# Squared scores of the first chunk stored unturned, read back in 256-byte pieces and turned in four later chunks

## The chip, the cores and the metric

One core of one Trainium2 chip runs the kernel. The metric is device time in microseconds (us); it is 1084.96 us before the change, the median of three runs (1084.34 to 1086.16).

## The reference, cut to what matters

Three layers follow each other over two samples of 3136 tokens. The change touches the first, an attention without softmax:

```python
def _attn_ref(u, v, z):                      # u, v: (2, 3136, 256), z: (2, 3136, 64)
    scale = 1.0 / S
    scores = scale * np.matmul(z, z.transpose(0, 2, 1))
    attn = np.maximum(scores, 0.0) ** 2
    out = np.matmul(attn, v)
    return (u * out).astype(np.float32)
```

Queries and keys are the same array z, so the squared scores are symmetric: the block of queries A against keys B is the turned block of queries B against keys A. Two dense layers with their own mixing follow (x + a low-rank mix, a two-layer net; a Fourier mix, a norm, a two-layer net). They take the second half of the time and are not touched.

## The kernel before, in words

The attention of a sample runs over 7 chunks of 448 queries, (b, qc) in the code. A chunk runs over 13 steps, one for each pair p of 128-key tiles (pair 12 holds the last 64 keys and is half a step). I write V(n) for the products of step n of a chunk and S(n) for its scores. A step needs its block of squared scores P, 128 x 896 in float32, and splits it in two parts, h (rounded) and l (the rest), which both enter the products with the values.

A step gets P in one of two ways.

- **Made**: `scores` runs 6 matmuls into psS (S(n)), ACT does Relu (L742) and Square (L743), ACT or DVE rounds h (L133 or L749), DVE subtracts l (L136).
- **Loaded**: `load_kept` loads a block that an earlier chunk stored, three steps ahead, from ACT's DMA queue (L669); `split_kept` rounds h on ACT (L133) and subtracts l on DVE (L136). No scores, Relu or Square.

A made step whose block a later chunk will load (I call it heavy) is turned by DVE in 32 x 32 blocks (`keep`, L688) one step later, and four DMAs write it to DRAM (L698), on POOL's and partly on SP's queue. `_kept` says which pairs of a chunk are loaded. Of sample 0, chunk 0 stores nothing, since its keys of pairs 0 and 1 are dealt to the two tiles in another way than elsewhere (`_plain`), so later chunks of sample 0 make pairs 0 and 1 again.

`_pairs` orders the 13 steps of a chunk: `places` gives the positions of the loaded pairs, the made ones fill the rest. `ahead(i + 2)` prepares the step two ahead of the one whose products `values(i)` runs, so on TensorE (PE) S(n + 2) stands before V(n). At a chunk's end `gate` copies the four accumulators psO (ACT L133, DVE L810), multiplies by u, turns the result once more (L817) and stores it; then PE runs two sets of scores in a row, S(1) and S(2) of the next chunk. Between the steps, conversion jobs of the weights run a few short instructions on DVE (L213, L214, then L219 to L221) and ACT (L216, L217); I call them the job's operations. Each engine runs its instructions in the order in which they stand.

Buffers rotate: P has 4 (`ptile`), `turned` has 5, psS has 2. A load goes to a `turned` buffer while fewer than two loads hold one, else to a P buffer.

Of the kernel before, what the change touches and what calls it, by code (L numbers as in the profile page):

```python
# [10 lines left out]
F32 = mybir.dt.float32  # L11
# [8 lines left out]
NB, S, D, DQK, RANK, DFF = 2, 3136, 256, 64, 32, 1024  # L20
N1, N2 = 64, 49
CH = 448
# [18 lines left out]
    return o1, o2, c1, c2, tok, feat  # L41


def _plain(b, p):
    return (b == 0) & (p < 2)


def _kept(b, qc):

    return [p for p in range(12) if 256 * (p + 1) <= qc * CH and (b or 256 * p >= CH)]  # L50


def _target(p, a):
# [12 lines left out]
def _pairs(b, qc):  # L66

    plain = [*range(6), 12, *range(6, 12)]
    if qc == 0:
        return plain  # L70
    kept = _kept(b, qc)
    made = [p for p in range(12) if p not in kept]
    heavy = [p for p in made if _stored(b, qc, p)]
    bare = [p for p in made if p not in heavy]

    def merged(x, y):
        at = [((k + 0.5) / len(z), n, v) for n, z in enumerate((x, y)) for k, v in enumerate(z)]
        return [v for _, _, v in sorted(at)]

    places = sorted([12, 7, 8, 3, 10, 5, 4, 9, 2, 11][: len(kept)])  # L80
    order = dict(zip(places, kept)) | {6: 12}
    rest = [n for n in range(13) if n not in order]
    order.update(zip(rest, bare[:2] + merged(bare[2:], heavy)))
    return [order[n] for n in range(13)]
# [38 lines left out]
def program(ctx, tc, zT, v, uT, U, V, w1a, w2a, w1b, w2b, b49, f64, fd, rep, mask, out):  # L123
    nc = tc.nc
    mm = nc.tensor.matmul
# [3 lines left out]
    load = nc.sync.dma_start  # L129
    late_dma = nc.gpsimd.dma_start  # L130
# [10 lines left out]
    dram = ctx.enter_context(tc.tile_pool(name="dram", bufs=1, space=DRAM))  # L141
# [4 lines left out]
    def ptile():  # L146
        return ctile("P", bufs=4)

    def c2(t):
        return t.rearrange("p (a n) -> p a n", a=2)  # L150

    def run(gen):
# [146 lines left out]
    class Chunk:  # L299
# [4 lines left out]
        def load(self):  # L304
            self.vs = com.tile([128, CH + 48], F32R, tag="Vs", name="Vs", bufs=1)[:, 0:CH]
            for k in (0, 64):
                late_dma(out=self.vs[k : k + 64, :], in_=V_d[:, self.sl])
# [178 lines left out]
    def attention(stack):  # L486
# [16 lines left out]
        def load_z(b, i, pairs=slice(0, 3)):  # L503

            raw = turned_tile()
            for j, r in enumerate(halves):
                if i < 4:
                    dma = late_dma if i == 0 or j and i > 1 else load
                    t0, n = 768 * i + 256 * pairs.start, pairs.stop - pairs.start
                    if _plain(b, 3 * i + pairs.start):  # L510
                        src = zT[b, :, t0 : t0 + 256 * n].rearrange("d (p j n) -> d j p n", j=2, n=128)
                        dma(out=raw[r, 0 : 128 * n].rearrange("d (p n) -> d p n", n=128), in_=src[:, j])
                    else:
                        dma(out=raw[r, 0 : 256 * n], in_=zT[b, :, t0 + j : t0 + j + 256 * n])
                else:
                    (late_dma if j else load)(out=raw[r, 0:64], in_=zT[b, :, S - 64 : S])
            zraw[b, i] = raw
# [24 lines left out]
        def split_z(b, i, pairs=slice(0, 3)):  # L542
            raw = zraw.pop((b, i))
            if b not in KT:
                KT[b] = big.tile([128, 12, 2, 128], F32R, tag="KT", name=f"KT_{b}")
            if i < 4:
                h, l = (KT[b][:, 3 * i : 3 * i + 3, k][:, pairs] for k in range(2))
                n = pairs.stop - pairs.start
                if _plain(b, 3 * i + pairs.start):
                    raw = raw[:, 0 : 128 * n].rearrange("d (p n) -> d p n", n=128)  # L550
                else:
                    raw = raw[:, 0 : 256 * n].rearrange("d (p n w) -> d p n w", n=128, w=2)[:, :, :, 0]
                (nc.vector.tensor_copy if (b, pairs.start) == (0, 2) else hcopy)(h, raw)
                sub(l, raw, f(h))
                return
            att.tile([128, 48], F32, tag="gap", name="gap", bufs=1)
            t = KTl[b] = att.tile([128, 2, 128], F32R, tag="KTl", name="KTl")
            for c in (0, 64):
                hcopy(t[:, 0, c : c + 64], raw[:, 0:64])
                sub(t[:, 1, c : c + 64], raw[:, 0:64], f(t[:, 0, c : c + 64]))  # L560
# [23 lines left out]
        def load_v(b, p):  # L584
            if b == 0 and order.index(p) % 4 in (0, 3) and p or b and last_order.index(p) % 4 > 1:
                raw = f(stage()[:, 0 : 2 * D]).rearrange("p (a n) -> p a n", a=2)
            else:
                raw = att.tile([128, 2, D], F32, tag="vraw", name="vraw")
            vraw[b, p] = raw
            if p < 12:  # L590
                how = "(a p) n -> p a n" if _plain(b, p) else "(p a) n -> p a n"
                load(out=raw, in_=v[b, p * 256 : p * 256 + 256, :].rearrange(how, a=2))
            else:
                for h in range(2):
                    load(out=raw[h * 64 : h * 64 + 64, 0, :], in_=v[b, S - 64 : S, :])
# [63 lines left out]
            for k in range(8):  # L659
                yield conv_w(w2a, k, True, wa[1])  # L660

        prob, kept, loads, writes, turns = {}, {}, [None, None], [], []

        def load_kept(b, qc, p):
            own = next((k for k in range(2) if loads[k] not in kept), None)
            A = kept[b, qc, p] = ptile() if own is None else turned_tile()
            if own is not None:
                loads[own] = b, qc, p
            nc.scalar.dma_start(out=c2(A), in_=kept_d[b, qc][256 * p : 256 * p + 256].rearrange("(m j) n -> m j n", j=2))  # L669

        def split_kept(b, qc, p):
            A, h, l = kept.pop((b, qc, p)), ctile("h", F32R), ctile("l", F32R)
# [6 lines left out]
        def keep():  # L679

            b, qc, p, A = turns.pop()
            t = turned_tile()
            rows = slice(qc * CH, qc * CH + CH)
            if p == 12:
                nc.vector.transpose(out=t[0:64, 0:CH], in_=A[0:64, 0:CH])
                n = 32
            else:
                nc.vector.transpose(  # L688
                    out=t.rearrange("p (b c j) -> p b j c", j=2, c=32),
                    in_=A.rearrange("p (j b r) -> p b j r", j=2, r=32),  # L690
                )
                n = 64
            def write():
                for k, (a, to, col) in enumerate(_stored(b, qc, p)):
                    t0, t1 = max(rows.start, 0 if b else 512), min(rows.stop, 256 * (to * CH // 256))
                    m0, m1 = (n * (x - rows.start) // 32 for x in (t0, t1))
                    if t1 > t0:
                        (load if k % 2 and qc < 3 else late_dma)(  # L698
                            out=kept_d[b, to][t0:t1, col : col + n].rearrange("(b r) k -> r b k", r=32),
                            in_=t[quads[a], m0:m1].rearrange("p (b k) -> p b k", k=n),  # L700
                        )

            writes.append(write)

        def scores(b, qc, p):
            ps = psS.tile([128, 2, 512], F32, tag="S", name="psS")
            extra = psO.tile([128, 512], F32, tag="O11", name="psO11") if (b, qc, p) == (0, 0, 0) else None
            q = Q[b, qc]

            w = CH if p < 12 else CH // 2  # L710
            for kk, kq in ((0, 0), (0, 1), (1, 0)):
                for j, r in enumerate(halves):
                    if p == 12:
                        k = KTl[b][r, kk]
                    elif (b, qc) == (0, 0) and p < 2:
                        c = 256 * p + 128 * j
                        k = q[r, kk, c : c + 128]
                    else:
                        k = KT[b][r, p, kk]
                    o = j * w if p == 12 else 0  # L720
                    if extra is None:
                        mm(ps[:, j, 0:w], k, q[r, kq, o : o + w], start=(kk, kq) == (0, 0), stop=kk == 1)  # L722
                    elif (kk, kq) == (0, 0):
                        dst = extra if j else ps[:, j]
                        mm(dst[:, 0:w], first_q[r, c : c + 128], first_q[r, 0:w], start=True, stop=True)
            A, h, l = ptile(), ctile("h", F32R), ctile("l", F32R)

            if (b, qc, p) == (0, 0, 0):
# [11 lines left out]
            else:  # L740
# [12 lines left out]
                    keep()  # L753
                if stored:
                    turns.append((b, qc, p, A))
            prob[b, qc, p] = (h, l)

        acc, heavy = {}, [0]
# [157 lines left out]
        first_q = qraw[0, 0]  # L916
# [6 lines left out]
        def ahead(i):  # L923
            if i < len(steps):
# [6 lines left out]
                    split_kept(b, qc, p)  # L931
                elif i:
                    scores(b, qc, p)
                if i + 3 < len(steps) and steps[i + 3][2] in _kept(*steps[i + 3][0:2]):
                    load_kept(*steps[i + 3])
                for write in done:
                    write()
                p = i % NP
# [482 lines left out]
```

## Time and profile before

| | |
|---|---|
| median of three runs | 1084.96 us (1084.34 to 1086.16) |
| profiled execution, its own time | 1086.77 us |
| its span, first to last instruction | 1085.0 us |
| PE busy | 1076.0 us, 99% of the span |
| DVE busy | 847.4 us, 78% |
| ACT busy | 623.7 us, 57% |
| POOL busy | 255.5 us, 24% |

The profiled execution took 1.81 us more than the median and has 1.77 us outside its span. The attention takes about the first 500 us, sample 0 the first 256. The granted TensorE clock is full throughout. DMA-issuing instructions are not counted as busy; in a timeline they stand under ACTq or SPq, the queues of ACT and SP.

### The profile page before, as it was taken

Reading aid. Unit: us, or ns where it says so; the run is one execution under the profiler, and the core shown is the slowest. Engines: PE = TensorE matmul, PEld = TensorE weight load, DVE = VectorE, ACT = ScalarE, POOL = GpSimd, SP = SyncE. Lnnn points to the kernel's source line nnn. Section 1 sums busy time; section 2 is a strip of 40 time slices with the busy share of each in tenths; the row PEclk is TensorE's granted clock in tenths of the full one; section 3 lists DMA queues with packets and bytes.
Section 4 is the critical chain, followed back from the end, with each engine's and each line's share of the span. In section 5 each row is a group of like instructions: output and inputs, shape, how many; then the busy total and the mean of one; then the engine's idle time right before and its main releaser. Section 6 shows DMA issues by size and latency. Waiting matters only on the chain.

```text
span 1085.0 us, 21199 instructions
## 1 busy us (share of the span) xinstructions
PE 1076.0 (99%) x7926; PEld 1004.9 (93%) x7926; DVE 847.4 (78%) x1571; ACT 623.7 (57%) x1094; POOL 255.5 (24%) x426
## 2 busy tenths in 40 slices
PE   9999999999999999999999999999999999999998
PEld 7999998999999999989899999999999999999997
DVE  7898888988999988665666776677687888778863
ACT  7888777777888876543433544443355454444431
POOL 2133344222443344221111121111231111011100
PEclk9999999999999999999999999999999999999999
DMA  6255577774667677875532553321253221121210
GB/s 175 74 155 159 154 207 209 244 247 129 192 183 192 190 249 214 294 240 160 168 79 77 152 169 103 78 75 36 66 125 105 62 90 47 35 66 46 60 43 35
DMA packets 140519, 146.04 MB, mean 135 GB/s; under 512 B 72534, under 2 KB 113530, under 8 KB 140416
## 3 DMA queue, kind: packets, MB, share of 16 engines
q1 hardware_dynamic: 108704, 70.57, 22.7%
q0 software_dynamic: 23280, 47.72, 15.6%
q10 hardware_dynamic: 8432, 26.40, 7.6%
q8 instruction: 62, 1.02, 0.4%
q14 instruction: 41, 0.34, 0.1%
HBM read 88.61 MB, written 56.00 MB: 133 GB/s over the span
## 4 chain that ended last, share of the span: by engine, by line
PE 89%; DMA 4%; DVE 3%; ACT 2%; issue 1%; POOL 1%; SPq 0%; DVEq 0%; ACTq 0%; POOLq 0%
PE psO L778 31%; PE psH L431 8%; PE psH L433 8%; PE psC L458 8%; PE psH L432 8%; PE psC L456 8%; PE psC L457 8%; PE psS L722 5%; DVE turned L688 1%; DVE l L136 1%; ACT P L742 1%; ACT P L743 1%; DMA vraw<-in_zT 0%; DMA vraw<-in_v 0%; DMA scr<-wst 0%
## 5 line engine op out<-in xcount | busy, mean ns | idle before, releaser
L778 PE MATMUL psO<-h,Vt 64*128 64x448 f32 x2744 | 318.5, 360 | 1.7 <-DVE h L749 1.2
L778 PEld LDWEIGHTS psO<-h,Vt 64*128 64x128 f32 x2744 | 265.3, 184 | 18.2 <-DVE h L749 3.8
L436 ACT ACTIVATE Hh<-psH 128x448 fp32r<-128x448 f32 x224 | 121.3, 543 | 243.2 <-PE psH L433 239.9
L437 DVE SCALAR_TENSOR_TENSOR Hl<-psH,Hh 128x448 fp32r<-128x448 f32 x224 | 137.8, 618 | 109.2 <-ACT Hh L436 107.4
L136 DVE TENSOR_TENSOR l<-P,h 128x896 fp32r<-128x896 f32 (+2 forms) x188 | 170.4, 913 | 51.6 <-ACT h L133 44.7
L778 PE MATMUL psO<-l,Vt 64*128 64x448 f32 x1372 | 180.9, 360 | 0.3
L431 PE MATMUL psH<-h,w 128*128 128x448 f32 x448 | 165.0, 368 | 0.0
L433 PE MATMUL psH<-h,w 128*128 128x448 f32 x448 | 162.5, 363 | 0.0
L458 PE MATMUL psC<-Hh,w 128*128 128x448 f32 x448 | 162.4, 363 | 0.0
L432 PE MATMUL psH<-l,w 128*128 128x448 f32 x448 | 162.3, 362 | 0.0
L457 PE MATMUL psC<-Hl,w 128*128 128x448 f32 x448 | 162.2, 362 | 0.0
L456 PE MATMUL psC<-Hh,w 128*128 128x448 f32 x448 | 162.1, 362 | 0.0
L698 POOL DMA_DIRECT2D kept<-turned x178 | 112.5, 637 | 156.8 <-DVE turned L688 124.1
L778 PEld LDWEIGHTS psO<-l,Vt 64*128 64x128 f32 x1372 | 135.8, 184 | 8.7 <-DVE l L136 2.5
L742 ACT ACTIVATE P<-psS 128x896 f32<-128x896 f32 (+1 forms) x124 | 107.9, 870 | 24.9 <-PE psS L722 23.8
L743 ACT ACTIVATE P<-P 128x896 f32<-128x896 f32 (+1 forms) x124 | 113.1, 912 | 3.9
L133 ACT CAST h<-P 128x448 fp32r<-128x448 f32 (+1 forms) x111 | 80.2, 733 | 56.9 <-DVE P L322 39.6
L431 PEld LDWEIGHTS psH<-h,w 128*128 128x128 f32 x448 | 84.1, 188 | 6.3 <-issue 0.3
L432 PEld LDWEIGHTS psH<-l,w 128*128 128x128 f32 x448 | 84.2, 188 | 5.7
L457 PEld LDWEIGHTS psC<-Hl,w 128*128 128x128 f32 x448 | 84.0, 188 | 5.9
L456 PEld LDWEIGHTS psC<-Hh,w 128*128 128x128 f32 x448 | 84.0, 187 | 5.8 <-issue 0.2
L458 PEld LDWEIGHTS psC<-Hh,w 128*128 128x128 f32 x448 | 84.0, 188 | 5.4
(299 smaller groups left out, 1354.5 us busy)
## 6 DMA issues: line engine op xcount, KB each, us to landing
turned<-kept ACTq DMA_DIRECT2D x49, 448.0 KB, 4.4
kept<-turned POOLq DMA_DIRECT2D x102, 112.0 KB, 3.6
uT<-in_uT SPq DMA_DIRECT2D x14, 448.0 KB, 7.0
out<-P SPq DMA_DIRECT2D x27, 224.0 KB, 1.9
aTd<-turned POOLq DMA_DIRECT2D x13, 448.0 KB, 3.6
kept<-turned SPq DMA_DIRECT2D x51, 112.0 KB, 3.0
aNd<-turned POOLq DMA_DIRECT2D x40, 112.0 KB, 3.6
scr<-wst SPq DMA_DIRECT2D x16, 256.0 KB, 2.0
```

The costliest lines, as they stand in the source:

```text
L136: tt(out=o, in0=a, in1=b, op=ALU.subtract)
L431: mm(ps[:, 0:CH], wh, self.h[:, a], start=a == 0, stop=False)
L432: mm(ps[:, 0:CH], wh, self.l[:, a], start=False, stop=False)
L433: mm(ps[:, 0:CH], wl, self.h[:, a], start=False, stop=a == 1)
L436: act(out=h, in_=ps[:, 0:CH], func=AF.Relu)
L437: stt(out=l, in0=ps[:, 0:CH], scalar=0.0, in1=f(h), op0=ALU.max, op1=ALU.subtract)
L456: mm(dst, wh, h, start=k == 0, stop=False)
L457: mm(dst, wh, l, start=False, stop=False)
L458: mm(dst, wl, h, start=False, stop=k == 7)
L742: act(out=A[:, x].rearrange("p (a n) -> p a n", a=2), in_=ps[:, :, 0:w], func=AF.Relu, scale=1.0 / S)
L743: act(out=A[:, x], in_=A[:, x], func=AF.Square)
L778: mm(o[fa][i][:, 0:CH], vt[r, j, k, fa * 128 : fa * 128 + 128], x[r, j * CH : j * CH + CH], start=n0 == 0 and fa not in [t[1][0] for t in ...
```

## The change

Chunk 0 of sample 0 now deals its keys like all others (even tokens to one tile, odd ones to the other; `_plain` goes, `dealt` reads with a stride of two) and stores the squared scores of pairs 3 to 10 as they are, unturned, in a DRAM array `first_d` (S x 448): eight DMAs of 448 KB on POOL's queue, each issued with the step after.

In chunks 2 to 5 of sample 0 (`LATE`) pairs 0 and 1 are loaded instead of made, eight steps in all (I call such a step U0 or U1). `load_kept` issues their loads four steps ahead, from ACT's queue: for U0 four DMAs of 32 partitions x 14 pieces x 256 bytes out of `first_d`; for U1 three of these and one of 32 partitions from the store of chunk 1, which now begins at query 448 and not 512. After the operations of the step before it, `turn_read` turns the pieces on DVE into a further P buffer (128 or 96 partitions x 896). Then the step goes on as a loaded one. The orders of these chunks change (b: made, not stored; h: heavy; k: loaded as before; U: loaded and turned):

```
chunk 2   before  b0 b1 h5 h6 b3 h7 h12 h8 h9 b4 h10 h11 k2
          now     b3 b4 h5 h6 h7 U0 h12 h8 U1 h9 h10 h11 k2
chunk 3   before  b0 b1 h7 b5 h8 h9 h12 k2 k3 h10 b6 h11 k4
          now     b5 b6 h7 k2 h8 h9 h12 U0 k3 h10 U1 h11 k4
chunk 4   before  b0 b1 h8 k2 h9 b7 h12 k3 k4 h10 k5 h11 k6
          now     b7 h8 h9 k2 k3 U0 h12 k4 U1 h10 k5 h11 k6
chunk 5   before  b0 b1 b8 k2 h10 k3 h12 k4 k5 b9 k6 h11 k7
          now     b8 b9 h10 k2 k3 U0 h12 k4 U1 k5 k6 h11 k7
```

The core of the diff:

```diff
+LATE = (2, 3, 4, 5)
+def _unturned(b, qc, p):
+    return b == 0 and qc in LATE and p < 2
 def _kept(b, qc):
-    return [p for p in range(12) if 256 * (p + 1) <= qc * CH and (b or 256 * p >= CH)]
+    return [p for p in range(12) if 256 * (p + 1) <= qc * CH and (b or 256 * p >= CH or qc in LATE)]
...
     places = sorted([12, 7, 8, 3, 10, 5, 4, 9, 2, 11][: len(kept)])
+    if _unturned(b, qc, 0):
+        others, at = kept[2:], {3: (0, 1), 5: (1, 3)}.get(len(kept), (2, 4))
+        for p, k in enumerate(at):
+            others.insert(k, p)
+        places = [5, 8, 12] if len(kept) == 3 else places
+        kept = others
...
+            n = (CH - rows.start) // 64 if p else 4
+            src = first_d[qc * CH : qc * CH + CH, rows.start : rows.start + 64 * n].rearrange("(b s) (q c) -> q s b c", s=32, c=64)
+            for q in range(n):
+                nc.scalar.dma_start(out=A[quads[q]].rearrange("s (b c) -> s b c", c=64), in_=src[q])
+            B = None
+            if n < 4:
+                B = ptile()
+                nc.scalar.dma_start(
+                    out=c2(B)[quads[3]], in_=kept_d[b, qc][rows][64 * n :].rearrange("(m j) n -> m j n", j=2)
+                )
+            unturned[b, qc, p] = B, slice(0, 32 * n)
+
+        def turn_read(b, qc, p):
+            B, r = unturned.pop((b, qc, p))
+            B = ptile() if B is None else B
+            nc.vector.transpose(
+                out=B[r].rearrange("p (j b s) -> p j b s", j=2, s=32),
+                in_=kept[b, qc, p][r].rearrange("p (b c j) -> p j b c", j=2, c=32),
+            )
+            kept[b, qc, p] = B
...
+                if b + qc == 0 and 256 * (p + 1) > LATE[0] * CH and 256 * p < (LATE[-1] + 1) * CH:
+                    dst = first_d[256 * p : 256 * p + 256].rearrange("(m j) n -> m j n", j=2)
+                    writes.append(lambda: late_dma(out=dst, in_=c2(A)))
...
-                if i + 3 < len(steps) and steps[i + 3][2] in _kept(*steps[i + 3][0:2]):
-                    load_kept(*steps[i + 3])
+                for s in steps[i + 3 : i + 5]:
+                    if s[2] in _kept(*s[0:2]) and _unturned(*s) == (s != steps[i + 3]):
+                        load_kept(*s)
+                if steps[i + 1 : i + 2] and steps[i + 1] in unturned:
+                    turn_read(*steps[i + 1])
```

How the instructions stand now, at three places. First ACT at the beginning of chunk 2, from the gate's second copy to the rounding of step 2 (h5). Before:

```order
L133 COPY turned<-psO_799 128x448
L742 ACTIVATE P<-psS 128x896
L743 ACTIVATE P<-P 128x896
L742 ACTIVATE P<-psS 128x896
L743 ACTIVATE P<-P 128x896
L133 CAST h<-P 128x896
```

Now:

```order
L142 COPY turned<-psO_808 128x448
L769 ACTIVATE P<-psS 128x896
L770 ACTIVATE P<-P 128x896
L678 DMA turned<-firstd 32x14x64 x4
L769 ACTIVATE P<-psS 128x896
L770 ACTIVATE P<-P 128x896
L142 CAST h<-P 128x896
```

The four issues for U0 have come between the Square of step 1 and the Relu of step 2.

Second DVE in the middle of chunk 2, from the turning of step 3's block (h6) to step 7 (h8); L713 and L710 turn a heavy block for storing, L690 turns a read one. Before:

```order
L688 STREAM_TRANSPOSE turned<-P 128x14x2x32
L749 CAST h<-P 128x896
L136 TENSOR_TENSOR l<-P,h 128x896 x2
L213 TENSOR_SCALAR stg<-stg 128x192
L214 TENSOR_SCALAR stg<-stg 128x192
L136 TENSOR_TENSOR l<-P,h 64x448
L688 STREAM_TRANSPOSE turned<-P 128x14x2x32
L685 STREAM_TRANSPOSE turned<-P 64x448
L749 CAST h<-P 128x896
L136 TENSOR_TENSOR l<-P,h 128x896
```

Now:

```order
L713 STREAM_TRANSPOSE turned<-P 128x14x2x32
L145 TENSOR_TENSOR l<-P,h 128x896
L690 STREAM_TRANSPOSE P<-turned 128x896
L145 TENSOR_TENSOR l<-P,h 128x896
L713 STREAM_TRANSPOSE turned<-P 128x14x2x32
L223 TENSOR_SCALAR stg<-stg 128x192
L224 TENSOR_SCALAR stg<-stg 128x192
L145 TENSOR_TENSOR l<-P,h 64x448
L710 STREAM_TRANSPOSE turned<-P 64x448
L776 CAST h<-P 128x896
L145 TENSOR_TENSOR l<-P,h 128x896
L690 STREAM_TRANSPOSE P<-turned 96x896
```

One rounding has gone and two turnings have come; the turning of h7 (the second L713) now stands ahead of the job's two operations.

Third ACT at the beginning of chunk 4, from the gate's second copy. Before:

```order
L133 COPY turned<-psO_1944 128x448
L742 ACTIVATE P<-psS 128x896
L743 ACTIVATE P<-P 128x896
L742 ACTIVATE P<-psS 128x896
L743 ACTIVATE P<-P 128x896
L133 CAST h<-P 128x896
L133 CAST h<-turned 128x896
```

Now:

```order
L142 COPY turned<-psO_1949 128x448
L769 ACTIVATE P<-psS 128x896
L770 ACTIVATE P<-P 128x896
L142 CAST h<-P 128x896
L673 DMA turned<-kept_78 128x896
L678 DMA P<-firstd 32x14x64 x4
L769 ACTIVATE P<-psS 128x896
L770 ACTIVATE P<-P 128x896
L142 CAST h<-P 128x896
L142 CAST h<-turned 128x896
```

The first two steps after the gate are now h8 and h9, both rounded on ACT, with five DMA issues between them.

## Rows read from the trace of the kernel before

**Rows 1.** Chunks 2 to 5: length; busy PE, PEld, DVE, ACT, POOL; clock, DMA share.

```profile
83.15:119.99 36.84, 36.73 (x368) 35.20 (x366) 32.28 (x47) 30.07 (x40) 11.86 (x18) 1.00 0.55 151
119.99:155.35 35.36, 35.36 (x356) 32.77 (x354) 29.98 (x49) 27.48 (x39) 17.05 (x27) 1.00 0.66 189
155.35:190.26 34.91, 34.65 (x345) 31.57 (x343) 29.15 (x48) 27.61 (x40) 15.71 (x26) 1.00 0.74 212
190.26:223.89 33.63, 33.63 (x338) 32.63 (x336) 30.59 (x51) 25.00 (x39) 9.27 (x15) 1.00 0.69 214
```

**Rows 2.** PE's timeline in chunk 2: start, length, operation.

```profile
92.59 0.77 PE L722 MATMUL psS<-Q,KT 64*128 64x448 f32 x6
93.19 1.79 PE L778 MATMUL psO<-h,Vt 64*128 64x448 f32 x16
...
95.62 0.49 PE L722 MATMUL psS<-Q,KTl 64*128 64x224 f32 x6
95.94 1.79 PE L778 MATMUL psO<-h,Vt 64*128 64x448 f32 x16
```

**Rows 3.** Groups of instructions, chunks 2 to 5: count, busy and mean, idle before.

```profile
L136 DVE TENSOR_TENSOR l<-P,h 128x896 fp32r<-128x896 f32 x33 | 35.9, 1092 | 8.7 <-ACT h L133 6.9
L743 ACT ACTIVATE P<-P 128x896 f32<-128x896 f32 x33 | 31.5, 954 | 1.0
L742 ACT ACTIVATE P<-psS 128x896 f32<-128x896 f32 x33 | 30.1, 911 | 4.9 <-PE psS L722 4.6
...
L133 ACT CAST h<-turned 128x896 fp32r<-128x896 f32 x15 | 13.9, 933 | 1.8 <-DMA turned<-kept 1.8
```

**Rows 4.** DVE's timeline at the start of chunk 2, from h5's l.

```profile
88.50 1.09 DVE L136 TENSOR_TENSOR l<-P,h 128x896 fp32r<-128x896 f32 x1 [1.01 <-ACT h L133]
89.51 0.35 DVE L219 SCALAR_TENSOR_TENSOR stg<-stg 128x192 int32<-128x192 int32 x1
...
90.44 1.10 DVE L817 STREAM_TRANSPOSE turned<-turned 128x896 f32<-128x896 f32 x1
91.47 1.07 DVE L688 STREAM_TRANSPOSE turned<-P 128x896 f32<-128x896 f32 x1
92.46 0.58 DVE L749 CAST h<-P 128x896 fp32r<-128x896 f32 x1
```

**Rows 5.** ACT's timeline at the start of chunk 2.

```profile
84.74 0.95 ACT L743 ACTIVATE P<-P 128x896 f32<-128x896 f32 x1
85.60 0.90 ACT L742 ACTIVATE P<-psS 128x896 f32<-128x896 f32 x1
```

**Rows 6.** ACT's timeline around the load of k2, late in chunk 2.

```profile
106.63 0.95 ACT L743 ACTIVATE P<-P 128x896 f32<-128x896 f32 x1
107.00 0.35 ACTq L669 DMA_DIRECT2D turned<-kept  x1
```

**Rows 7.** DMA issues: L822 in 256-byte pieces; L669's waits, loads and landings.

```profile
L822 SPq DMA_DIRECT2D aNd<-turned x12: 302/402/664, 53.4 to 373.6; - x12
...
L669 ACTq EVENT_SEMAPHORE  x79: 17/38/3872, 106.6 to 483.1; - x79
...
DMA to landing us min/median/max: 3.1/5.3/7.5
```

**Rows 8.** SP's queue around the start of chunk 4.

```profile
147.40 8.77 SPq L632 DMA_DIRECT2D stg<-in_V  x2
156.28 1.76 SPq L569 DMA_DIRECT2D qraw<-in_zT  x2
```

**Rows 9.** DMA queues, packets, MB and share: 46 to 83 us, then 120 to 156.

```profile
q1 hardware_dynamic: 8901, 2.73, 28.9%
...
q10 hardware_dynamic: 576, 1.84, 16.5%
```

**Rows 10.** ACT in chunk 0: Square of pair 3, and a split of keys.

```profile
16.83 0.96 ACT L743 ACTIVATE P<-P 128x896 f32<-128x896 f32 x1
...
24.11 0.53 ACT L133 CAST KT<-turned 128x384 fp32r<-128x384 f32 x1
```

More of the change, by code (lines that the diff above doesn't have):

```diff
@@ L41, in _orders @@
     return o1, o2, c1, c2, tok, feat
-def _plain(b, p):
-    return (b == 0) & (p < 2)
+LATE = (2, 3, 4, 5)
+def _unturned(b, qc, p):
+    return b == 0 and qc in LATE and p < 2
 def _kept(b, qc):
-    return [p for p in range(12) if 256 * (p + 1) <= qc * CH and (b or 256 * p >= CH)]
+    return [p for p in range(12) if 256 * (p + 1) <= qc * CH and (b or 256 * p >= CH or qc in LATE)]
 def _target(p, a):
@@ L167, in program @@
     }
+    first_d = dram.tile([S, CH], F32, tag="firstd", name="firstd")
     V_d = dram.tile([2 * RANK, S], F32R, tag="Vd", name="Vd")
@@ L509, in load_z @@
                     t0, n = 768 * i + 256 * pairs.start, pairs.stop - pairs.start
[L510 to L514, printed above, removed]
+                    dma(out=raw[r, 0 : 256 * n], in_=zT[b, :, t0 + j : t0 + j + 256 * n])
                 else:
@@ L548, in split_z @@
                 n = pairs.stop - pairs.start
[L549 to L552, printed above, removed]
+                raw = raw[:, 0 : 256 * n].rearrange("d (p n w) -> d p n w", n=128, w=2)[:, :, :, 0]
                 (nc.vector.tensor_copy if (b, pairs.start) == (0, 2) else hcopy)(h, raw)
@@ L590, in load_v @@
             if p < 12:
-                how = "(a p) n -> p a n" if _plain(b, p) else "(p a) n -> p a n"
-                load(out=raw, in_=v[b, p * 256 : p * 256 + 256, :].rearrange(how, a=2))
+                load(out=raw, in_=v[b, p * 256 : p * 256 + 256, :].rearrange("(p a) n -> p a n", a=2))
             else:
@@ L660, in conversions @@
                 yield conv_w(w2a, k, True, wa[1])
-        prob, kept, loads, writes, turns = {}, {}, [None, None], [], []
+        prob, kept, loads, writes, turns, unturned = {}, {}, [None, None], [], [], {}
         def load_kept(b, qc, p):
@@ L668, in load_kept @@
                 loads[own] = b, qc, p
-            nc.scalar.dma_start(out=c2(A), in_=kept_d[b, qc][256 * p : 256 * p + 256].rearrange("(m j) n -> m j n", j=2))
+            rows = slice(256 * p, 256 * p + 256)
+            if not _unturned(b, qc, p):
+                nc.scalar.dma_start(out=c2(A), in_=kept_d[b, qc][rows].rearrange("(m j) n -> m j n", j=2))
+                return
+            n = (CH - rows.start) // 64 if p else 4
[17 more added lines that the diff above has]
+            kept[b, qc, p] = B
         def split_kept(b, qc, p):
@@ L694, in write @@
                 for k, (a, to, col) in enumerate(_stored(b, qc, p)):
-                    t0, t1 = max(rows.start, 0 if b else 512), min(rows.stop, 256 * (to * CH // 256))
+                    t0, t1 = max(rows.start, 0 if b else CH if to in LATE else 512), min(rows.stop, 256 * (to * CH // 256))
                     m0, m1 = (n * (x - rows.start) // 32 for x in (t0, t1))
@@ L703, in keep, with dealt @@
             writes.append(write)
+        def dealt(x, j):
+            return x.rearrange("d (n w) -> d n w", w=2)[:, :, j]
         def scores(b, qc, p):
@@ L715, in scores @@
                     elif (b, qc) == (0, 0) and p < 2:
-                        c = 256 * p + 128 * j
-                        k = q[r, kk, c : c + 128]
+                        k = dealt(q[r, kk, 256 * p : 256 * p + 256], j)
                     else:
@@ L724, in scores @@
                         dst = extra if j else ps[:, j]
-                        mm(dst[:, 0:w], first_q[r, c : c + 128], first_q[r, 0:w], start=True, stop=True)
+                        mm(dst[:, 0:w], dealt(first_q[r, 0:256], j), first_q[r, 0:w], start=True, stop=True)
             A, h, l = ptile(), ctile("h", F32R), ctile("l", F32R)
```

## The prediction

> **What bounds the kernel now.** I read the page first: PE is busy 99% of the span. Then the busy time by chunk: in chunks 2 to 5, the only ones whose steps change, PE is busy 140.4 of 140.74 us at full clock, DVE 122.0, ACT 110.2 [rows 1]. PE's timeline gives the grid: one set of scores takes 0.60 us, one set of products 2.43, of which the first 1.6 need h alone, half a step's scores 0.33 [rows 2]. So a made step costs PE 3.0 us, a loaded one 2.4. With 12 whole steps, pair 12 (0.33 and 0.6) and 11, 9, 7 and 6 sets of scores, the four chunks would take 36.3, 35.1, 33.9 and 33.3, in all 138.7; they take 140.74 [rows 1]. So 2.0 us are stalls already. Last I read the other queues step by step: they show how little lead PE's inputs have. h6 is rounded at 92.46 to 93.04, and its products start at 93.19 [rows 2, 4].
>
> **What it removes.** Eight sets of scores: 8 x 0.60 = 4.8 us of PE. Ideal lengths fall to 35.1, 33.9, 32.7 and 32.1, in all 133.9. ACT loses eight Relus and Squares (0.91 + 0.95) and gains eight roundings at 0.93 [rows 3]. DVE loses eight roundings, 0.65 from start to start, and gains eight turnings, 1.03, as the like L688 (91.47 to 92.46, 90.44 to 91.47) [rows 4].
>
> **What it adds to the queues.** ACT issues 32 DMAs. The nearest rows: 0.35 for a load's issue, 0.40 for an SP issue in the same 32 x 14 x 64 pieces, at most 0.66 [rows 6, 7]. A single issue costs ACT nothing: it lies inside the Square that runs from 106.63 to 107.58 [rows 6]. Four take 1.6 us, and cover ends after the Square. I take 0.4 each, hence 0.7 to 0.8 us on ACT per read; bounds are 0 (wholly covered) and 1.8 (0.66 each). A waiting issue also holds back what is behind it on ACT: L669 has waited up to 3.87 us [rows 7].
>
> Behind the turning stands a chain that a made step hasn't got: DVE turns (1.03), ACT rounds (0.93), DVE subtracts (1.01). ACT is tied to DVE's place there, while the next Relu stands behind the rounding. DVE's queue has 18.7 us idle in these chunks, but the waits fall where loaded steps crowd and PE moves at 2.4 a step.
>
> **The walk.** I put the four chunks on the grid, zero where PE starts two sets of scores (83.15, 119.99, 155.35, 190.26), and let each engine run its new order with the durations of rows 3 and 4, half-size operations at 0.6 (an estimate, a bit over half). A stall is how much later h (or l) is ready than PE needs it.
>
> Chunk 2. The Square of step 1 starts at 1.6 (84.74), and Relu of h5 followed at 2.45 (85.60) [rows 5]; U0's four issues now come between, so it starts at 3.25. h5's l was at 5.35 (88.50), goes to 6.1; behind it on DVE stand the job (0.93), the gate's turning (1.03), h5's (0.99), and then h6's rounding [rows 4], ready at 10.65. PE wants it at 9.6, since no S(5) stands ahead: stall 1.05. Next, the turning of U0 ends at 14.8, ACT rounds until 15.7 and does pair 12's half-size work until 17.4; then the job's two operations on ACT wait for DVE's, which now stand behind U0's l and h7's turning, until 18.2. So h8's Relu starts at 18.95 and h is ready at 21.4; PE wants it at 20.05: 1.35. Next, h9's Relu needs the P buffer that U1 gives free with its l, at 25.5; h is ready at 28.3 instead of 27.45: 0.85. h10, behind the job on ACT, 31.85 for 30.7: 1.15. h11, behind h10's turning on DVE, 0.65, and its l 0.25. In all 5.3.
>
> Chunk 3 (U0 stands behind pair 12, U1 next to last): h of U0 0.2, h10 0.4, U1 0.7 (turned at 26.4, rounded 27.4, wanted 26.7), h11 0.8, its l 0.2: 2.3.
>
> Chunk 4. h8 and h9 come first and both are rounded on ACT, with five issues between; h9's Relu goes from 3.6 to 4.65, h to 7.4, wanted at 6.0: 1.4. There is more here: in the built program DMAs of SP and ACT take eight completion semaphores in turn, and an issue waits until the DMA eight back has landed. For U0's third and fourth piece these are SP's second stg<-in_V, issued just before 156.17, and qraw at 156.28 [rows 8]; with the 5.3 of a median landing [rows 7] the third is free near 160.7, 5.3 on the grid, and ACT some 1.3 later than I counted: 2.7. Then pair 12 0.2, U1 1.05, h10 0.95, h11 0.1: 5.0.
>
> Chunk 5, where k2 k3 U0 h12 k4 U1 stand in a row: h10 0.65 (issues), U0 0.55, pair 12 0.35, k4 0.85, U1 1.2: 3.6. DVE needs about 15 us in the 13 that PE gives these steps.
>
> Sum: 5.3 + 2.3 + 5.0 + 3.6 = 16.2 of stalls on 133.9 makes 150.1, for 140.74 now: +9.4. In chunk 0, POOL's second half of the last keys' load stands behind a write that waits for pair 3's Square (17.79); with 5.3 to land it comes near 24.2, wanted at 24.11 [rows 7, 10]: +0.3, bounds 0 and 2 (a landing at 7). The eight writes overtake their P buffers, which come round every four steps, some 10 us. I rounded each of about 20 links up by some 0.04 (0.8) and trust the SP landing by half (0.7). So I take +8: 1086.77 + 8 = 1094.8 in the profiled execution's own time, and as that lies 1.81 above the median, 1093.0. With ACT's issues at nothing 2.5 of stalls and the 1.3 go: 1089.2 from there; at 0.66 each, some 3 to 4 more: 1097.
>
> **Rivals.**
> - The gain comes through: stalls stay at 2.0 to 4.6, since issues overlap the ACT work and the turnings fill the idle 18.7 us of DVE. Time 1080.2 (1085.0 - 4.8) to 1082.8. For it: averages leave room (DVE would be at 125 of 136, ACT lower). Against: waits of ACT for DVE are in the chain already, and PE's margin at h6 is 0.15 us. It decides if the 16.2 are overcounted by a factor of 3.5. Chance 0.21.
> - Half: stalls of 4.6 to 9 cancel the gain. 1082.8 to 1087.1. Chance 0.13.
> - Late reads: the 256-byte pieces land after their turning should start. A packet of 307 bytes takes 19.3 ns (28.9% of 16 engines x 37 us over 8901), one of 3.2 KB 165 ns [rows 9], so a read of 1792 pieces is 2.2 us of all engines against 1.5 for a plain load. From the first issue the walk leaves 9 us at the least, landings took 5.3 and at most 7.5 [rows 7]. If each landed at 10, eight waits of 1 us come on top: 1101. Chance 0.05. The Trainium skill (DMA: Bandwidth & Descriptors, Specifications) wants at least 512 bytes for a transfer at line rate, below which the engine reads, modifies and writes; 15.9 GB/s an engine here against 19.4 show a fifth lost, not half. If half were lost, a read would be an estimated 3 us of all engines and would still be in time.
> - The forecast, DVE and ACT late for PE: 1087.1 to 1098, chance 0.61.
>
> The Trainium skill (DMA: Bandwidth & Descriptors, Anatomy of one DMA) has any semaphore wait happen on the issuing sequencer ahead of dispatch; the 3.87 us of L669 on ACT's queue agree. If the wait lay in the DMA engines instead, the 1.3 of chunk 4 would go: 1092.
>
> **How the numbers follow.** 0.2% is 2.2 us, about what a measurement of this kernel can tell from no change: faster is below 1082.8, slower above 1087.1. Faster 0.21, same 0.13, slower 0.61 + 0.05 = 0.66. The likeliest case has 1087.1 to 1098 as its own range, 1093.0 as its value; the range for 8 in 10 goes down into the first rival, to 1081.5, and up to 1098.
>
> **What would show it.** In the changed profile chunk lengths near 40, 36, 37 and 35.5 where PE's idle time is put down to h (L133, L749) and l; PE's scores with 48 matmuls fewer; Relu of the first heavy step after the gate 0.7 us or more behind the Square in chunks 2, 4 and 5; ACT's roundings of U waiting for the turnings, not the turnings for DMA. I am wrong if the chunks come to 35.5, 34.2, 33.5 and 32.5 (then ACT's issues cost nothing and DVE's idle time took the rest), or if the turnings wait for landings.

## The result and the profile after

The changed kernel takes 1099.95 us (median of 4, 1099.40 to 1100.51) against 1084.70 (4 runs of before on the same chip): a ratio of 1.0137, 95% interval 1.0125 to 1.0150. It is slower, as forecast, but by 15.25 us, not 8, and the time lies 2 us above the upper end of the range. The profiled execution took 1099.99, so here it stands at the median, not 1.8 above it as that of before did.

Chunks 2 to 5 (L749 is the scores' line now, before L722; L142 and L145 are the helper lines L133 and L136; L713 was L688, L769 and L770 were L742 and L743, L776 was L749), length, busy time of PE, PEld, DVE, ACT, POOL, granted clock and DMA share, as [rows 1]:

```profile
82.40:123.82 41.42, 38.24 (x356) 34.10 (x354) 33.52 (x47) 28.19 (x38) 11.54 (x18) 0.96 0.61 169
123.82:161.97 38.15, 35.35 (x344) 31.39 (x342) 30.80 (x49) 25.86 (x37) 15.87 (x26) 1.00 0.68 185
161.97:201.42 39.45, 35.03 (x332) 32.46 (x330) 30.00 (x48) 25.69 (x38) 16.34 (x27) 0.96 0.73 212
201.42:237.48 36.06, 33.61 (x326) 29.91 (x324) 31.12 (x51) 23.27 (x37) 8.26 (x15) 1.00 0.76 228
```

In all 155.08. For before [rows 1] gives 140.74, but there chunk 2 is counted from 83.15, and PE's timeline, by which every other start is read, has its two sets of scores earlier:

```profile
82.99 1.37 PE L722 MATMUL psS<-Q,KT 64*128 64x448 f32 x12
```

So chunk 2 took 37.00 before and the four 140.90, and the change costs them 14.18. The work is what the prediction counted: PE has 1358 matmuls in the records for the 1407 of [rows 1], DVE is 125.4 and ACT 103.0 us busy. What is new is that PE waits. Its timeline, the steps with the largest waits in brackets:

```profile
93.93 2.48 PE L808 MATMUL psO<-h,Vt 64*128 64x448 f32 x16 [1.76 <-DVE h L776]
...
144.15 1.87 PE L808 MATMUL psO<-h,Vt 64*128 64x448 f32 x16 [1.81 <-ACT h L142]
...
172.81 2.80 PE L808 MATMUL psO<-h,Vt 64*128 64x448 f32 x16 [4.42 <-ACT h L142]
208.59 1.88 PE L808 MATMUL psO<-h,Vt 64*128 64x448 f32 x16 [1.00 <-DVE h L776]
...
224.17 1.87 PE L808 MATMUL psO<-h,Vt 64*128 64x448 f32 x16 [0.99 <-ACT h L142]
```

Each waits for an h, and two engines make it late. First ACT's queue at the head of chunks 2 and 4. In [rows 5] the next Relu followed the Square within 0.9; now U0's four issues stand between, 2.00 us long in chunk 2 and 4.69 in chunk 4:

```profile
84.15 0.95 ACT L770 ACTIVATE P<-P 128x896 f32<-128x896 f32 x1
84.31 2.00 ACTq L678 DMA_DIRECT2D turned<-firstd  x4
86.42 0.92 ACT L769 ACTIVATE P<-psS 128x896 f32<-128x896 f32 x1 [1.31 <-DMA turned<-firstd]
```
```profile
164.73 0.33 ACTq L673 DMA_DIRECT2D turned<-kept  x1
165.09 4.69 ACTq L678 DMA_DIRECT2D P<-firstd  x4
169.89 0.92 ACT L769 ACTIVATE P<-psS 128x896 f32<-128x896 f32 x1 [4.23 <-DMA qraw<-in_zT]
```

Second, ACT waits for the turnings (L690). Its rounding of P, in the groups of chunks 2 to 5, with the idle time ahead of it, and DVE's subtraction (8.7 of idle in [rows 3]):

```profile
L145 DVE TENSOR_TENSOR l<-P,h 128x896 fp32r<-128x896 f32 x34 | 37.1, 1091 | 19.1 <-ACT h L142 17.9
...
L142 ACT CAST h<-P 128x896 fp32r<-128x896 f32 x21 | 19.8, 942 | 21.8 <-DVE P L690 10.0 <-DMA turned<-firstd 7.5 <-PE psO L808 4.0
```

The 7.5 is put down to a transfer, but DVE did not wait for one ahead of its turnings (no idle time in their groups), so it too was waiting for DVE:

```profile
L690 DVE STREAM_TRANSPOSE P<-turned 96x896 f32<-96x896 f32 x3 | 3.2, 1075 | 0.0
```

Twice the granted clock fell to half, after PE had stood for 1.76 and 4.42 us; windows of 2 us behind the first:

```profile
92.00:94.00 2.00, 0.23 (x4) 0.07 (x2) 1.90 (x4) 1.94 (x3) 1.33 (x2) 1.00 0.29 75
94.00:96.00 2.00, 2.00 (x16) 1.81 (x18) 2.00 (x2) 0.51 (x1) 1.33 (x3) 0.75 0.70 192
96.00:98.00 2.00, 2.00 (x16) 1.80 (x14) 2.00 (x3) 0.00 (x0) 1.23 (x2) 0.50 1.11 310
```

### The profile page after: what moved, and what is told of

Same layout as the page of the kernel before. It is cut to its first block, busy times and chain, and to the rows that moved or that the text cites. A ratio compares the mean times of both kernels' runs of the same rounds, so it can differ in the third digit from the quotient of the medians.

```text
span 1098.2 us, 21149 instructions
## 1 busy us (share of the span) xinstructions
PE 1077.1 (98%) x7878; PEld 1000.3 (91%) x7878; DVE 851.2 (78%) x1571; ACT 616.7 (56%) x1086; POOL 259.0 (24%) x434
## 4 chain that ended last, share of the span: by engine, by line
PE 78%; DVE 1%; DMA 0%; ACT 0%; issue 0%; DVEq 0%
PE psO L808 22%; PE psH L441 8%; PE psH L443 8%; PE psC L468 8%; PE psC L466 8%; PE psH L442 8%; PE psC L467 8%; PE psS L749 3%; PE ps_m L1214 0%; DMA stg<-in_w1a 0%; PE ps_g L1214 0%; PE ps_x L1214 0%; PE psS L292 0%; PE ps_g L292 0%; DVE turned L713 0%
## 5 line engine op out<-in xcount | busy, mean ns | idle before, releaser
L145 DVE TENSOR_TENSOR l<-P,h 128x896 fp32r<-128x896 f32 (+2 forms) x189 | 171.7, 915 | 62.5 <-ACT h L142 56.0
L142 ACT CAST h<-P 128x896 fp32r<-128x896 f32 (+1 forms) x120 | 88.7, 749 | 79.6 <-DVE P L332 39.6
L769 ACT ACTIVATE P<-psS 128x896 f32<-128x896 f32 (+1 forms) x116 | 100.8, 869 | 25.5 <-PE psS L749 18.7
L770 ACT ACTIVATE P<-P 128x896 f32<-128x896 f32 (+1 forms) x116 | 105.5, 909 | 3.7
```

What stands on the lines that cost most here:

```text
L145: tt(out=o, in0=a, in1=b, op=ALU.subtract)
L770: act(out=A[:, x], in_=A[:, x], func=AF.Square)
```

## The experiments

All are edits of the changed kernel. The chunk lengths come from one profile each, counted from where PE starts its first double set of scores; the last column is the 95% interval of the ratio to before. One profile is less firm than the ratio: chunk 4 took 34.50 us in the run with turnings two steps ahead and 36.44 in a later one in which its steps are the same (`LATE = (3, 4)`).

| kernel | chunk 2 | 3 | 4 | 5 | sum | median us | ratio |
|---|---|---|---|---|---|---|---|
| before | 37.00 | 35.36 | 34.91 | 33.63 | 140.90 | 1084.7–1085.8 | 1 |
| changed | 41.42 | 38.15 | 39.45 | 36.06 | 155.08 | 1099.95 | 1.0125–1.0150 |
| reads on SP | 40.01 | 38.32 | 35.15 | 35.25 | 148.73 | 1093.47 | 1.0055–1.0085 |
| one issue on ACT | 40.04 | 37.97 | 36.81 | 34.47 | 149.29 | 1093.47 | 1.0052–1.0086 |
| four issues of whole rows | 41.20 | 37.95 | 39.31 | 35.84 | 154.30 | 1100.03 | 1.0113–1.0144 |
| Q load earlier | 41.42 | 38.12 | 39.25 | 36.16 | 154.95 | 1099.01 | 1.0110–1.0140 |
| no turning | 39.44 | 35.82 | 40.10 | 34.78 | 150.14 | 1094.25 | 1.0063–1.0101 |
| one issue, no turning | 37.64 | 34.31 | 34.04 | 32.74 | 138.73 | 1084.15 | 0.9976–0.9997 |
| order alone | 37.54 | 36.00 | 34.57 | 33.84 | 141.95 | 1087.59 | 1.0009–1.0028 |
| SP, DVE rounds U | 39.75 | 37.78 | 35.31 | 37.88 | 150.72 | 1094.48 | 1.0065–1.0095 |
| SP, roundings swapped | 39.78 | 37.80 | 35.49 | 37.58 | 150.65 | 1094.69 | 1.0072–1.0103 |
| ACT reads, turned two ahead | 39.67 | 38.41 | 40.36 | 34.71 | 153.15 | 1097.47 | 1.0090–1.0121 |
| SP, turned two ahead | 37.40 | 35.18 | 34.50 | 33.76 | 140.84 | 1086.28 | 1.0002–1.0021 |
| SP, turned three ahead | 38.39 | 36.30 | 36.45 | 42.12 | 153.26 | 1095.53 | 1.0065–1.0109 |

**Is it the issues on ACT, the turnings, or the order?** Four runs. Reads on SP (`load` is SP's):

```
             for q in range(n):
-                nc.scalar.dma_start(out=A[quads[q]].rearrange("s (b c) -> s b c", c=64), in_=src[q])
+                load(out=A[quads[q]].rearrange("s (b c) -> s b c", c=64), in_=src[q])
...
-                nc.scalar.dma_start(
+                load(
                     out=c2(B)[quads[3]], in_=kept_d[b, qc][rows][64 * n :].rearrange("(m j) n -> m j n", j=2)
```


> The changed kernel with U0's and U1's reads issued on SP, not on ACT. Issue theory (the reads hold ACT's queue, by their own 0.5 us each and by the semaphores that they wait for): the stall at h6 of chunk 2 (2.14) and the one at the head of chunk 4 (4.80) nearly go, and with them both drops of the clock; chunks 2 to 5 fall from 155.1 to about 146, time near 1091. Turning theory (DVE turns, ACT rounds, DVE subtracts, and what stands behind waits): these stalls stay but for 2 us, time near 1098. Landing theory: later pieces, 1100 or more.

No turning (the plain quarter is read into A too):

```
         def turn_read(b, qc, p):
-            B, r = unturned.pop((b, qc, p))
...
-            kept[b, qc, p] = B
+            unturned.pop((b, qc, p))
```

> The changed kernel with the eight turnings on DVE left out: U0 and U1 go on unturned, so the result is another one. Issue theory: the two large stalls stay, the smaller ones of chunks 3 and 5 shrink, 4 to 5 us in all, time near 1095. Turning theory: the chunks fall to about 141, time near 1086. Landing theory: ACT's rounding of U now waits for the transfer itself, time near 1100.

Order alone (and no writes of the first chunk's squares):

```
-    return [p for p in range(12) if 256 * (p + 1) <= qc * CH and (b or 256 * p >= CH or qc in LATE)]
+    return [p for p in range(12) if 256 * (p + 1) <= qc * CH and (b or 256 * p >= CH)]
...
     kept = _kept(b, qc)
+    if _unturned(b, qc, 0):
+        kept = [0, 1] + kept
```

> Pairs 0 and 1 of chunks 2 to 5 are made by scores as before the change, but at the places that the change gives U0 and U1; no first-chunk squares are stored or read. Issue theory and turning theory: the order itself costs little, 1084 to 1087. Order theory (loaded steps and heavy steps crowd wherever the new places are): half of the loss is here already, 1090 or more.

One issue:

```
-            for q in range(n):
-                nc.scalar.dma_start(out=A[quads[q]].rearrange("s (b c) -> s b c", c=64), in_=src[q])
...
+            t0 = qc * CH + 192 * p
+            nc.scalar.dma_start(out=c2(A), in_=first_d[t0 : t0 + 256].rearrange("(m j) n -> m j n", j=2))
```


> The changed kernel with each of the eight reads made by one issue on ACT, 256 whole rows of 1792 bytes of the same stored squares, in place of three or four issues of 256-byte pieces (the values are other ones, so the result is too); the turning stays. Issue theory: as with the issues on SP or better, 146 us for the chunks, time near 1090. Turning theory: 1097. Landing theory: near 1092 too, and ACT or DVE no longer waits for a transfer.

Both suspects count. Taking the issues from ACT gives back 6.35 us of the chunks by SP, 5.79 by one issue; leaving out the turnings 4.94; the order costs 1.0 against before (2.0 by the ratio). The issue theory was 2.5 to 3.5 us too hopeful in the first and last run, the turning theory 8 in the second. Both edits together:

> One issue of whole rows for each read, and the turning left out too (other values, so another result): both suspects gone, U0 and U1 are as cheap as any loaded step. If the issues and the turnings are the whole loss beside the order: chunks 2 to 5 near 138 (133.9, the 1.2 that the order alone cost, some 3 for crowding), time near 1083. If loaded steps that follow each other at 2.4 us are themselves the limit (ACT rounds them, DVE subtracts them): 142 to 145, time 1087 to 1090.

138.73: 16.35 come back, 5.6 more than the single gains of 5.79 and 4.94 add up to. By the ratios the three gains are 16.3, 7.4 and 6.0 us, an excess of 2.9, and as each ratio is uncertain by 1 to 2 us, that is not clear of noise. A likely reason for it, not tested by itself: h hangs on ACT and DVE in turn, so with one of them still late the other's gain is partly waited away. Below before this version is by 0.13% at the median, less than the 0.2% set as measurable, and it computes something else.

**What in the issues costs?** The prediction put 1.3 us of chunk 4 down to semaphores that U0's third and fourth issue share with SP's loads. Freed:

```
-                    if p == 4:
+                    if p == (2 if (b, qc) == (0, 4) else 4):
                         load_q(*nxt)
```


> The changed kernel, with one thing moved: in chunk 4 the load of the next Q stands two steps earlier in SP's program, so that U0's third and fourth read take completion semaphores of transfers that have long landed; no work is added or left out. Semaphore theory: ACT's four issues there fall from 4.69 to near 2.0, the stall of 4.80 to 1.5 or less, the drop of the clock behind it goes, chunk 4 from 39.45 to 35.5 to 36.5, time near 1096.5. If the four issues are slow for another reason (their own work on 256-byte pieces, the crowded DMA engines): chunk 4 stays above 38.5, time near 1099.5.

ACT's timeline in chunk 4 there:

```profile
164.31 0.33 ACTq L673 DMA_DIRECT2D turned<-kept  x1
164.68 4.50 ACTq L678 DMA_DIRECT2D P<-firstd  x4
169.28 0.92 ACT L769 ACTIVATE P<-psS 128x896 f32<-128x896 f32 x1 [4.03 <-issue]
```

The semaphore theory falls: the transfers it blamed were issued at 152.8 to 154.3, and the four issues still took 4.50 (the wait of the Relu is now put down to "issue", not to a DMA). It is the issues themselves that are long, in the changed kernel too (shortest, median and longest in ns):

```profile
L678 ACTq DMA_DIRECT2D P<-firstd x4: 310/1198/1492, 165.1 to 169.5; - x4
```

The semaphore events of the traces show what is left of the theory. In the changed kernel the DMA eight back had landed at 167.08 when the third issue began at 167.79; for the fourth it landed at 169.45, and that issue began at 169.47, after a wait of 0.4. In the runs without turning and with whole rows such waits take 1.8 and 1.2 us, the issues are shorter, and the four together take 4.50 and 4.54 all the same. So the semaphores do hold issues here, but freeing them does not shorten the four. Then the pieces:

```
-            nc.scalar.dma_start(out=c2(A), in_=first_d[t0 : t0 + 256].rearrange("(m j) n -> m j n", j=2))
+            for q in range(4):
+                rows = first_d[t0 + 64 * q : t0 + 64 * q + 64]
+                nc.scalar.dma_start(out=c2(A)[quads[q]], in_=rows.rearrange("(m j) n -> m j n", j=2))
```

> As the run with one issue on ACT, but four issues for each read, each of 64 whole rows of 1792 bytes (other values, another result); turning one step ahead. If an issue costs by itself, whatever its pieces: four take about 2.0 us, up to 4.7 in chunk 4, the stall there stays above 3, time near 1099. If the 256-byte pieces make it long: four take about 1.4 us, also in chunk 4, time near 1094.

```profile
164.35 0.33 ACTq L673 DMA_DIRECT2D turned<-kept  x1
164.72 4.54 ACTq L678 DMA_DIRECT2D P<-firstd  x4
```

The 256-byte pieces are innocent: four issues of 1792-byte rows took 1.77 in chunk 2 and 4.54 in chunk 4, and the time did not move. With a single issue ACT's row in chunk 4 is this:

```profile
163.12 0.53 ACTq L676 DMA_DIRECT2D P<-firstd  x1
```

It is the number of issues, at the same place of the chunk (3.1 us from its start in both). Each took 0.44 to 0.50 at the head of chunk 2; why the four of chunk 4 take 4.5 to 4.7 in every run that has them on ACT (five of five), while chunk 5's take 2.06 with the DMA engines nearly as busy (0.83 against 0.89 in the stretch of the issues), stays open. Issued by SP they start at 154.59, ten microseconds earlier, and take 2.10.

**DVE's load, or the place in its queue?** With the reads on SP ACT still stood idle 18.7 us for turnings:

```profile
L142 ACT CAST h<-P 128x896 fp32r<-128x896 f32 x21 | 19.8, 941 | 20.6 <-DVE P L690 18.7 <-PE psO L808 1.5
```

U0 of chunk 3 shows why (same run, DVE, ACT and PE in order of start):

```profile
139.29 0.62 DVE L145 TENSOR_TENSOR l<-P,h 64x448 fp32r<-64x448 f32 x1 [1.41 <-ACT h L142]
...
140.16 1.11 DVE L713 STREAM_TRANSPOSE turned<-P 128x896 f32<-128x896 f32 x1 [0.26 <-DMA kept<-turned]
...
141.31 1.11 DVE L690 STREAM_TRANSPOSE P<-turned 128x896 f32<-128x896 f32 x1
142.51 0.94 ACT L142 CAST h<-P 128x896 fp32r<-128x896 f32 x1 [2.55 <-DVE P L690]
...
143.50 1.88 PE L808 MATMUL psO<-h,Vt 64*128 64x448 f32 x16 [1.97 <-ACT h L142]
```

The turning stands behind pair 12's l, which waits for ACT, and behind the turning of a pair to be stored. The data is there; DVE comes too late. Four runs tell place from load. h of U rounded on DVE:

```
-            hcopy(h, A)
+            (nc.vector.tensor_copy if _unturned(b, qc, p) else hcopy)(h, A)
```


> Reads issued on SP, and h of U0 and U1 rounded on DVE right behind the turning, not on ACT. In the run with the reads on SP alone ACT stood idle 18.7 us ahead of these roundings, for DVE's turnings, with the next Relu queued behind them. Queue theory (ACT's blocked queue is what makes the later h late): these waits go, the stalls of PE put down to ACT's h (6.7 us in chunks 2 to 5) mostly go, chunks 2 to 5 from 148.7 to 142 or 143, time near 1088. Load theory (DVE has too much to do): DVE gets 5.2 us more, the chunks stay at 147 or more, time 1092 or more.

and, besides, 12 of DVE's 13 whole roundings given to ACT (the last stays on DVE):

```
-                swift = stored and heavy[0] % 3 and p != pairs_of[b, qc][-1]
+                swift = (stored and heavy[0] % 3 or b == 0 and qc in LATE) and p != pairs_of[b, qc][-1]
```

> As the run before, and in return ACT rounds h of the 13 whole made pairs of chunks 2 to 5 that DVE rounded: DVE near 122 us, ACT near 107. Queue theory with a share of load: chunks near 139 to 141, time 1084 to 1086, at the kernel before. If ACT is late now, since its queue holds Relu, Square and rounding of every made pair: 145 or more, 1091 or more.

Neither brought time back: the chunks took 2 us more. ACT's 18.7 us of idle went, as the queue theory had it, but PE then waited for DVE's roundings of U (L698 there) in the same places:

```profile
L808 PEld LDWEIGHTS psO<-h,Vt 64*128 64x128 f32 x784 | 73.1, 185 | 20.1 <-DVE h L698 8.6 <-DVE h L776 3.5 <-ACT h L142 3.2
```

And with DVE 8 us lighter (122.4 for 130.3) the chunks took the same 150.65. So ACT's blocked queue alone is not the cause, and moving DVE's load to ACT is no cure; as ACT got 11.4 us busier by it, load is not ruled out by this run. What is left is where the turning stands:

```
-                if steps[i + 1 : i + 2] and steps[i + 1] in unturned:
-                    turn_read(*steps[i + 1])
+                if steps[i + 2 : i + 3] and steps[i + 2] in unturned:
+                    turn_read(*steps[i + 2])
```


> Reads issued on SP as they were, but each turning stands two steps ahead of its use on DVE, not one; ACT rounds U0 and U1 as in the changed kernel. Queue theory: ACT no longer waits for the turnings (18.7 us of idle to under 6), chunks 143 to 145, time 1088 to 1090. Landing theory: the read is now turned 5 to 6 us after its issue, DVE waits for the transfer and everything behind it is late: 150 or more, time 1095 or more.

140.84, 7.9 us less than with the reads on SP alone (6.4 by the ratios), and it is an effect of place only: the same operations on the same engines. U0 of chunk 3 again:

```profile
133.49 1.10 DVE L690 STREAM_TRANSPOSE P<-turned 128x896 f32<-128x896 f32 x1
...
137.15 0.93 ACT L142 CAST h<-P 128x896 fp32r<-128x896 f32 x1
137.22 1.11 DVE L713 STREAM_TRANSPOSE turned<-P 128x896 f32<-128x896 f32 x1
...
138.16 1.96 PE L808 MATMUL psO<-h,Vt 64*128 64x448 f32 x16
```

No bracket is left, and in the whole run no turning waited for a transfer: the landing theory fell too. (Its profiled execution was the fastest of ten; the median is 1.1 us above it.) The same move with the reads left on ACT:

> The changed kernel with only the turnings moved, from one step ahead of use to two; the reads stay on ACT. If issue and turning each add their own: the 7.9 us that the same move was worth with the reads on SP, chunks 155.1 to 147, time near 1092. If ACT's held queue keeps the loss by itself, as it did with the turning left out: 150, 1094. Landing theory: DVE now waits for the transfers, 153 or more, 1097 or more.

Only 1.9 us came back (3.4 by the ratios): the issues still hold ACT, PE stands 1.70, 1.90 and 4.29 us in chunks 2, 3 and 4. One step further (`i + 3` in place of `i + 2`, SP reads) the place turns against itself:

> Reads on SP, each turning three steps ahead of its use. With two steps ACT still waited 7.4 us for turnings and chunks 2 to 5 took 140.8. If the place of the turning in DVE's queue is the cause: that wait goes to under 2, the chunks to 138.5 to 140, time 1083 to 1085. If the tiles of P, held one step longer, or the landings take over: the chunks at 142 or more, 1087 or more.

ACT's wait for turnings went, but DVE now waited ahead of three turnings, 6.5 us in all, and everything behind was late. (This profile is 2.4 us above its median.) What ended DVE's idle time before L690:

```profile
  DMA P<-firstd: 2.5, 1
  DMA vraw<-in_zT: 2.2, 1
  DMA turned<-firstd: 1.8, 1
```

With two steps, and DVE relieved by the same line on `swift`:

> Reads on SP, turnings two steps ahead, and ACT rounds h of the 13 whole made pairs that DVE rounded. If DVE's load still matters once the turnings stand early enough: 138.5 to 140 for the chunks, 1083 to 1085. If only the order mattered: 140.8, or 1 to 2 more since ACT's queue gets longer; 1086 to 1088.

142.28, 1.0026 (1.0013 to 1.0039): relieving DVE (117.1 us busy for 124.3) gained nothing while ACT grew to 114.5 from 103.0, and the longer queue on ACT cost at most a little.

**Turning in chunk 0 instead** (the second run with the places that sample 1 uses):

```
-    return b == 0 and qc in LATE and p < 2
+    return False
...
-    return [(a, *_target(p, a)) for a in range(4) if _target(p, a)[0] > qc]
+    return [(a, *_target(p, a)) for a in range(4) if _target(p, a)[0] > qc and (b or qc or _target(p, a)[0] in LATE)]
```

> Chunk 0 turns its squares on DVE and stores them in the kept form, in the pieces that other chunks use, all by POOL; chunks 2 to 5 load U0 and U1 by one plain issue and turn nothing, at the places of the change. Same result as the changed kernel. Issue and turning theories: chunks 2 to 5 as in the run with one issue and no turning; chunk 0, where DVE had 3.2 us of 30.3 free, loses 4 to 6 us to eight turnings of 1.03. Time 1087 to 1092. If chunk 0 hides the turnings: 1083.

> As the run before, but U0 and U1 stand where the rule of sample 1 puts loaded pairs, spread among the made ones, not at the places of the change. If the places of the change crowd the loaded steps: 1 to 3 us below the run before. If the places are indifferent: the same within 1 us.

1.0043 (1.0030 to 1.0057) and 1.0050 (1.0035 to 1.0065). Chunks 2 to 5 fall to 137.18 (138.25 with the other places, so the change's own places do not crowd), 3.7 below before, but they begin at 90.72, 7.7 later. Chunk 0, where DVE was busy 26.9 of 30.3 us before, cannot hide eight turnings; PE's waits there include these, under half of the 7.7:

```profile
30.22 1.88 PE L805 MATMUL psO<-h,Vt 64*128 64x448 f32 x16 [0.85 <-DVE h L776]
37.75 1.88 PE L805 MATMUL psO<-h,Vt 64*128 64x448 f32 x16 [0.92 <-DVE h L776]
47.81 1.07 PE L805 MATMUL psO<-h,Vt 64*128 64x448 f32 x8 [1.51 <-DVE h L776]
```

**Chunk 0's part and a version that pays.** The list of late chunks empty (`LATE = ()`):

> The changed kernel with the list of late chunks empty: only the plain order of the first keys in chunk 0 stays, nothing is stored, read or turned late, and chunks 2 to 5 run in the order of before. If the 0.75 us by which the changed kernel reaches chunk 2 earlier comes from chunk 0's own edit: 0.5 to 0.8 below before, ratio 0.9993 to 0.9995. If it comes from chance in one profile: ratio 1.0000. If the new order of loads delays the keys (the prediction's +0.3): 1.0003.

1.0005 (0.9996 to 1.0013): no difference shown, and chunk 2 began at 83.11 (82.99 before). With the eight writes in chunk 0 it began at 81.49 to 83.00 in the profiles, but at 82.83 too in the run of the order alone, which has no writes; what brings it forward was not followed up. Last, two steps ahead on SP with `LATE = (3, 4, 5)` (six writes in chunk 0, not eight) and `LATE = (3, 4)`:

> The version with reads on SP and turnings two steps ahead, with chunk 2 left as before (it made U0 and U1 again, 36.84 against 37.40 there). If the chunks keep their lengths apart: 36.84, 35.18, 34.50, 33.76, in all 140.3, and chunk 0 with six writes fewer to pay for than eight: 0.5 to 1.0 below before, ratio 0.9990 to 0.9995. If no version of the change pays: 1.0005 to 1.0015.

> The same with chunks 3 and 4 alone reading U0 and U1, the two that came out shorter than before (35.18 against 35.36, 34.50 against 34.91): chunks 2 to 5 near 140.1, ratio 0.9990 to 0.9995. If no version pays: 1.0000 to 1.0010.

1.0015 (1.0006 to 1.0024) and 1.0000 (0.9991 to 1.0009). No version of the change beats the kernel before; the best undo the loss.

## Why the prediction was right in direction and wrong in size

- **Right:** PE loses its 4.8 us of scores, and more than that comes back as waits for h because ACT's issues and the chain from DVE's turning to ACT's rounding make it late. That chunks 2 and 4 are the worst was right, and it is not the landings: the late reads rival fell with the run of whole rows and with the turnings two steps ahead.
- **The step that failed is the walk.** It gave chunks of 40.4, 36.2, 37.7 and 35.7, in all 150.1; they took 155.08. Three of its links were mis-sized. *Issues at 0.4 each*: they took 0.50, and with the gaps around them the Relu of h5 came at 4.0 on the grid, not 3.25 (0.16 of it is the grid's zero of 83.15, which should be 82.99); h of h6 followed 0.8 late, and its stall was 1.76, not 1.05. *U0 of chunk 3, 0.2*: the walk let ACT and DVE go on, where DVE first waited 1.42 us for pair 12's h and then turned the stored pair; the stall was 1.81. *h9 of chunk 4, 2.7*: the four issues took 4.69, not 1.6 + 1.3, and the stall was 4.42. All that hangs on ACT's issues was put at 3.8 us (1093.0 against 1089.2 with issues at nothing); taking them from ACT gave back 6.35. The walk also left the clock at full.
- **The semaphores** of that last link were read rightly and priced wrongly: the third issue's came free at 5.1 on the grid (5.3 in the prediction), but the first two issues ran until 5.8 by themselves, so it held nothing; the fourth waited 0.4, and freeing both changed the four issues by 0.19 us. What makes the issues long there stays open.
- **The haircut** of 1.5 for rounding and for the SP landing went the wrong way: the walk as it stood was already 5.0 short. The forecast also counted from a profiled execution 1.81 above its median, and that of the changed kernel lies at its own: of the 7.0 us missing 5.2 show in the profiled times, and 1.8 are this difference.
- **Chunk 0, +0.3**: not borne out; no effect is shown either way. **The order**, which the walk did not price by itself, cost 1.0 (2.0 by the ratio).

The Trainium skill (DMA: Bandwidth & Descriptors, Issuing engines are not separate DMA queues) says that DMAs of all issuers share the same engines, so that moving one to another issuer saves only the sequencer's time to start it, usually small beside the transfer. No run here tests the first half. The second agrees with the trace as far as the transfer goes (0.5 us for the median issue, 6.2 from issue to landing where the trace gives it), but what the issue holds back in its own queue can count for more: started by SP, ACT's 28 issues from firstd and four more from kept gave back 6.35 us.

## What to carry to other kernels

Price a DMA's issue on the queue of the engine that also computes, by the number of issues and not by bytes: here four issues ahead of a Relu on the path cost two microseconds or more, with rows of 1792 bytes as with pieces of 256, and on SP's queue, which computes nothing, they held up no computation. An operation that feeds a loaded step must stand in its engine's queue by the time its reader is free, with the transfer's landing as the limit on the other side; of the three tried here two steps ahead was best, one cost 7.9 us more and three 12.4 (6.4 and 8.2 by the ratios). When two engines hand a value back and forth, also take both causes away together: here that gave back 16.35 us, each alone 5 to 6.

## What was not expected of the hardware

Four issues in a row on ACT took 1.7 to 2.2 us in the other places (the three pieces of chunk 5's U1 2.3 to 2.7) and 4.5 to 4.7 in chunk 4, in five kernels, with whole rows as with small pieces and also, in the one run that freed them, with the semaphores free. PE's granted clock fell to 0.50 of full speed (1.2 of 2.4 GHz) behind each of the five stalls of 4.2 to 4.4 us there, but only behind some of 1.7 to 2.0: chunk 2 shows 0.96 in the changed kernel after 1.76 of standing, and 1.00 in the run with the Q load earlier after 1.75. Both took 41.42 us, so there the slow stretch cost nothing; PE went on to wait anyway. What it cost in chunk 4 was not measured by itself; an estimate is 1.6 us at most, since the step behind the stall took 4.09 us there (172.81 to 176.90) and 2.52 at full clock in the run with the Q load earlier (93.55 to 96.07).
